# Two convolutions back to back in every second block of a fused convolution and squared-ReLU kernel

## The chip, the cores and the metric

The kernel runs on one core of a Trainium2 chip. The time is device microseconds (us) of one launch. Five engines work beside each other, each on its own in-order stream: PE (TensorE, the matmuls), ACT (ScalarE), DVE (VectorE), POOL (GpSimd) and SP (here only a queue that issues transfers). They wait for each other through semaphores. "PEld" in the profile is PE's loading of weights, which overlaps its matmuls.

## The reference, cut to what matters

Input `x` is 8 x 4096 x 192. A weight of its own for every token, head and tap (8 heads, 7 taps) goes through a softmax over the taps and then weights the token and its six predecessors (a causal dynamic convolution). The result passes through a feed-forward layer with squared ReLU.

```
w = exp(weight_gen - max);  w = w / (sum(w) + 1e-9)      # over 7 taps
out = einsum('bshk,bskhg->bshg', w, x_unf)               # x_unf: 7 shifted copies of x
h = maximum(out @ w_in, 0)                               # 192 -> 2048
y = (h * h) @ w_out                                      # 2048 -> 192
```

## The kernel before, in words

The 32768 tokens are 64 sub-blocks of 512 (`TB`). A block is two sub-blocks, apart from the first two, which are one each: 33 blocks, numbered from 0, in `BLOCKS`. A block passes through these steps.

- **Softmax pieces** (steps "E" and "S", class `Softmax`, lines 190 to 279). One batch, eight sub-blocks, is normalized at a time and in four pieces of rows, cut by `CUTS` at 0, 8, 18, 28 and 38. ACT takes the exponentials (line 238), DVE the sum, the reciprocal and the scaling (lines 245, 252, 260), and the result goes to DRAM. `TIMES` and the default in line 767 say at which unit of which block each piece is put: for a batch whose first block is `f`, at unit 9 of the blocks f-5 to f-2.
- **Rows and x** (`load_rows`, `x_load`). SP's queue loads the normalized rows (`wr`) of a block two blocks ahead; POOL's queue loads `x` (`xt`) of a block right after the conv of the block before it has been issued.
- **Bands** (step "B", `st_bands`, line 391). DVE multiplies the rows with a 0/1 mask to a banded matrix `bd`, with which the convolution becomes a matmul. A sub-block's band is one or two instructions; in block j the bands for block j+1 are made ahead of units 1 and 5.
- **Conv** (step "C", `st_conv_spread` from the ninth block on, line 464). 80 matmuls of 128 rows by 32 columns write two PSUM tiles `yp` of two banks each, 40 matmuls a tile; the first is copied to `y` by ACT, the second by DVE (line 495). Four small transfers on SP's queue then move pieces of `y` into place (line 499).
- **Units** (step "u", `st_unit`). A block has 16 units. One unit is six matmuls of 64 rows by 128 columns (line 564) into a PSUM tile `h`, a ReLU by ACT into `t1` (line 578) and a squaring by DVE into `g` (line 582). Units are squared in pairs, the last two of a block singly.
- **Second matmul** (step "M", `st_mm2`, line 613). A step is 32 matmuls: half of the 2048 inner channels for 256 tokens. Eight steps make a block. After every second step ACT copies one bank of the sum (line 627), DVE adds the other (line 629) and SP stores. The M steps of a block run while the units of the next block run: its first step needs the squares of units 0 to 7, its second those of units 8 to 15, in this order.

All tiles `yp` and `h` come from one PSUM ring of three (`ps_h`, line 89): a tile can be written when the tile three before it has been read out. The two banks of the second matmul's sum (`ps_o`) exist once: the next sum starts when DVE's addition of the last one is done.

The order is written out by hand. From the ninth block on every block follows

```
steady_spread = "MuMuuu" * 2 + "MuCMuuu" + "MuMuuu"
```

where "C" is the conv of the next block. `fill` puts the pieces E, S, B and L (load of weights) ahead of a unit. Instructions stand on each engine in the order in which these steps issue them.

Of the kernel before, what the change touches and what calls it, by code (L numbers as in the profile page):

```python
# [9 lines left out]
def kernel(  # L10
# [26 lines left out]
    nc = tc.nc  # L37
    f32 = mybir.dt.float32
    f16 = mybir.dt.float16

    B, S, D = x.shape
    H, KK = weight_gen.shape[2], weight_gen.shape[3]
# [3 lines left out]
    G = D // H  # L46
    SPREAD = H - 2
    FIRST_SPREAD = 8
    HP = H // 2

    P = 128
# [10 lines left out]
    SL = 8  # L62
# [15 lines left out]
    p_wg = ctx.enter_context(tc.tile_pool(name="p_wg", bufs=2))  # L78
    p_one = ctx.enter_context(tc.tile_pool(name="p_one", bufs=1))
    p_sm = ctx.enter_context(tc.tile_pool(name="p_sm", bufs=2))  # L80
    p_x = ctx.enter_context(tc.tile_pool(name="p_x", bufs=2))
    p_wr = ctx.enter_context(tc.tile_pool(name="p_wr", bufs=4))
    p_bd = ctx.enter_context(tc.tile_pool(name="p_bd", bufs=3))
    p_y = ctx.enter_context(tc.tile_pool(name="p_y", bufs=2))
    p_t1 = ctx.enter_context(tc.tile_pool(name="p_t1", bufs=3))
    p_g = ctx.enter_context(tc.tile_pool(name="p_g", bufs=14))
    p_os = ctx.enter_context(tc.tile_pool(name="p_os", bufs=2))
# [10 lines left out]
    mask = const.tile([P, P, 2], f16, name="mask")  # L98
    FIRST = 8
    NSEL = TB + TB - P + FIRST - 1 + P  # L100
    sel = const.tile([P, NSEL], f16, name="sel")
    PARTS = {0: (8, 8, 8, 8), 1: (8, 8, 16), 2: (16, 16)}
    v_big = const.tile([P, R + 2 * HALO, HP, SL, 2], f16, name="v_big")
    v_first = [
        const.tile([P, FIRST + 2 * HALO, HP, SL, 2], f16, name=f"v_first{i}") for i in (0, 1)
    ]

    def row_select():
# [214 lines left out]
    def x_load(j):  # L323
        x_t[j] = p_x.tile([P, NT, D], f16, name="xt")
        block_load(j, x_t[j], x[j // NBB], D, nc.gpsimd)
# [55 lines left out]
    def st_band(j, tiles):  # L381


        if j not in bd_t:
            bd_t[j] = p_bd.tile([P, H * NT * STEP], f16, name="bd")
        i = tiles[0]
        lo = STEP * i
        shift = 0 if i == 0 and j % NBB == 0 else lo - tile_start(j, i)
        n = min(STEP, P - shift)
        shape = (P, HP * len(tiles), n // SL, 2 * SL)  # L390
        nc.vector.tensor_tensor(  # L391
            out=bd_t[j][:, H * lo : H * (lo + len(tiles) * n)].rearrange(
                "p (g m c) -> p g m c", g=shape[1], c=2 * SL
            ),
            in0=wr_t[j][:, i : tiles[-1] + 1]
            .rearrange("p t g c -> p (t g) c")
            .unsqueeze(2)
            .broadcast_to(shape),
            in1=mask[:, shift : shift + n]
            .rearrange("p (m c) e -> p m (c e)", c=SL)  # L400
            .unsqueeze(1)
            .broadcast_to(shape),
            op=AluOp.mult,
        )
# [56 lines left out]
        else:  # L461
            nc.scalar.copy(out=y[:, 0:2], in_=yp)

    def st_conv_spread(j):

        s0, n = BLOCKS[j]
        y = p_y.tile([P, NK + 1, TB], f16, name="y")
        y_t[j] = y
        for ks in ((NK, NK - 1), (0, 1)):
            yp = ps_h.tile([P, 2, TB], f32, name="yp", tag="h")  # L470
            k0 = min(ks)
            for k in ks:
                for i in range(NT):
                    a, b = bounds[i], bounds[i + 1]
                    for half in (0, 1):
                        s = s0 + half
                        hi = a + (STEP if tile_start(s, i) == starts[i] else b - a)
                        bd = bd_t[s][:, H * a : H * hi].rearrange(
                            "p (g c e) -> p g e c", g=HP, e=2
                        )  # L480
                        for e in (0, 1):
                            head = 2 * k + e
                            p0 = RT * half + 32 * e
                            c0 = min(G * head, D - 32)
                            nc.tensor.matmul(  # L485
                                out=yp[p0 : p0 + 32, k - k0, a:b],
                                lhsT=x_t[s][:, i, c0 : c0 + 32],
                                rhs=bd[:, head // 2, e, 0 : b - a],
                                start=True,
                                stop=True,  # L490
                                skip_group_check=True,
                                tile_position=(0, p0),
                            )
            copy = nc.vector.tensor_copy if k0 == 0 else nc.scalar.copy
            copy(out=y[:, k0 : k0 + 2], in_=yp)  # L495
        for p0 in range(0, P, 32):
            head = SPREAD + p0 // 32 % 2
            r0 = p0 + G * head - min(G * head, D - 32)
            nc.sync.dma_start(out=y[p0 + G : p0 + 32, 0:NK], in_=y[r0 : r0 + G, NK])

    def st_conv(j):

        if j >= FIRST_SPREAD:
            return st_conv_spread(j)
        if j < NFIRST:
            return st_conv_first(j)
        y = p_y.tile([P, NK, TB], f16, name="y")
        y_t[j] = y
        yps = [ps_h.tile([P, 2 * TB], f32, name="yp", tag="h") for _ in range(2)]
        for later, s, i, q, half, a, b, base in conv_pieces(j):  # L510
            lo = bounds[i]
            hi = lo + (STEP if tile_start(s, i) == starts[i] else bounds[i + 1] - lo)
            _, ha, hb, pre = quads[q]
            m, h = (32, hb) if later else (pre, ha)
            bd = bd_t[s][:, H * lo : H * hi].rearrange("p (g c e) -> p g e c", g=HP, e=2)
            p0 = RT * half + 32 * (q % 2)
            k = q // 2
            col = TB * (k % 2) - base
            nc.tensor.matmul(  # L519
                out=yps[k // 2][p0 : p0 + m, col + a : col + b],  # L520
                lhsT=x_t[s][:, i, 32 * q : 32 * q + m],
                rhs=bd[:, h // 2, h % 2, a - lo : b - lo],
                start=True,
                stop=True,
                skip_group_check=True,
                tile_position=(0, p0),
            )
        for n, yp in enumerate(yps):
            k0, k1 = 2 * n, min(2 * n + 2, NK)
            nc.scalar.copy(  # L530
                out=y[:, k0:k1],
                in_=yp[:, 0 : (k1 - k0) * TB].rearrange("p (k c) -> p k c", c=TB),
            )
# [114 lines left out]
    with nc.allow_low_precision("fp16 matmul pipeline"), tc.manual_schedule():  # L648
# [15 lines left out]
            for j in range(first, first + P * s.r // TB):  # L664
                wr_load_sbuf(j, near, range(NT), engines)

        warm = const.tile([P, TB], f16, name="warm")
        gate = const.tile([P, 1], f32, name="gate")
        nc.vector.memset(warm, 0.0)
        nc.vector.memset(sel, 0.0)  # L670
# [43 lines left out]
        for q in range(4):  # L714
# [7 lines left out]

        steady = "MuMuuu" * 3 + "MuuuMCu"
        steady_spread = "MuMuuu" * 2 + "MuCMuuu" + "MuMuuu"
        plans = {
            0: "B1 u u u u E1 C S1 u u M u u",
            1: "L3 u u B2 M E2 B3 u M E2 u u S2 S2 u M u C u M",
# [8 lines left out]
        def at(j, u, kind, *args):  # L736
            fill.setdefault((j, u), []).append((kind, *args))
# [8 lines left out]
            (2, 0): ((6, 1), (6, 15), (7, 0)),  # L746
            (2, 1): ((7, 9), (8, 9)),
            (3, 0): ((9, 9), (10, 0), (10, 9), (11, 9)),
        }

        def exp_time(j, u):

# [10 lines left out]
        for n, s in enumerate(parts[4:], 4):  # L763
            b, f = s.b, s.fb
            k = n - min(m for m, p in enumerate(parts) if p.b == b)
            times = TIMES.get((b, k)) or (
                (f - 5, 9), (f - 4, 9), (f - 3, 9), (f - 2, 9)
            )
            assert len(times) == len(s.pieces)
            for j, u in times:  # L770
                at(*exp_time(j, u), "E", n)
                at(j, u, "S", n)
            at(times[0][0] - 1, 0, "L", n)
        for j in range(len(plans), NBLK - 1):
            a = BLOCKS[j + 1][0]
            small = [p for p in parts if p.fb <= j + 1][-1].r == FIRST
            us = {4: (7, 9), 6: (7, 9)}.get(j, (5, 9) if small else (1, 5))
            if j + 1 >= FIRST_SPREAD:
                us = (1, 5)
            for n, u in enumerate(us):  # L780
                at(j, u, "B", a + n)
        for j in range(len(plans), NBLK):
            plan, u = [], 0
            for step in steady_spread if j + 1 >= FIRST_SPREAD else steady:
                if step == "u":
                    plan += [f"{kind}{n}" for kind, n in fill.get((j, u), ())]
                    u += 1
                plan.append(step)
            plans[j] = " ".join(plan)
# [51 lines left out]

        mm2 = quarters()
        for j in range(NBLK):
            if j + 2 < NBLK:
                load_rows(j + 2)
            if j == 1:
                for q in range(WQ):
                    cross_w_in(q)
# [1 line left out]
            for step in plans[j].split():  # L850
# [4 lines left out]
                elif kind == "M":  # L855
                    next(mm2)
                elif kind == "C" and j + 1 < NBLK:
                    st_conv(j + 1)
                    if j == 0:
                        x_load(3)  # L860
                    elif j + 2 < NBLK:
                        for k in range(BLOCKS[j + 2][0], sum(BLOCKS[j + 2])):
                            x_load(k)
                    if j == 5:
                        load_w_spread()
                    elif j == 6:
# [56 lines left out]
```

The softmax here doesn't subtract the row's maximum and nothing guards it: scores larger than these inputs give would overflow.

## Time and profile before

| | us |
|---|---|
| median of three runs (732.42 to 733.91) | 733.32 |
| the profiled execution, its own time | 733.26 |
| span of the profiled execution | 731.5 |
| PE busy | 724.6 |
| DVE busy | 626.1 |
| ACT busy | 612.8 |
| POOL busy | 100.0 |

The page of the profile lists busy time by engine, the chain of work that ended last, and the costliest groups of instructions: line, engine, operation, output and input tile with their shapes, count, busy time, the mean of one, and the idle time before them with what ended it. The timeline lists merged instructions in order of time: start, duration, engine, line, tiles, count, and in brackets the idle time just before. Idle time of an engine that does not set the end costs nothing.

### The profile page before, as it was taken

What the parts mean: (1) busy time and instruction counts of PE and PEld (TensorE: products, weight loads), DVE (VectorE), ACT (ScalarE), POOL (GpSimd) and SP (SyncE); (2) the same over time, 40 slices, a digit from 0 to 9 for tenths busy, and PEclk for the clock granted to TensorE, in tenths of its full rate; (3) what the DMA queues carried; (4) which work ended last, traced back from release to release, by engine and by line L of the source; (5) the groups of instructions that cost most, each with busy time, mean ns of one, the idle gap of its engine ahead of it and who ended that gap; (6) DMA issues with size and microseconds to landing.
All of it is one profiled execution on the core that took longest, in us unless ns stands there. A gap on an engine that the chain in (4) does not pass through costs nothing.

```text
span 731.5 us, 30985 instructions
## 1 busy us (share of the span) xinstructions
PE 724.6 (99%) x14053; PEld 529.2 (72%) x14053; DVE 626.1 (86%) x834; ACT 612.8 (84%) x731; POOL 100.0 (14%) x145
## 2 busy tenths in 40 slices
PE   8999999999999999999999999999999999999998
PEld 4557788777777777777777777777777777777777
DVE  6898998998898988888988888988889988778753
ACT  5999888888888888888888888888888888888883
POOL 8232222321001100011000010010000110001000
PEclk9999999999999999999999999999999999999999
DMA  9555444784445452455433554334544315444012
GB/s 204 115 105 115 82 76 109 146 150 118 98 66 136 87 94 57 86 117 114 72 69 68 124 116 87 56 73 120 103 87 86 57 50 120 66 87 78 30 45 68
DMA packets 125984, 68.30 MB, mean 93 GB/s; under 512 B 85321, under 2 KB 122140, under 8 KB 125340
## 3 DMA queue, kind: packets, MB, share of 16 engines
q0 software_dynamic: 46192, 19.43, 22.5%
q1 hardware_dynamic: 79516, 46.79, 22.5%
q8 instruction: 110, 1.80, 1.0%
q14 instruction: 22, 0.18, 0.1%
q10 hardware_dynamic: 144, 0.10, 0.0%
HBM read 50.18 MB, written 28.70 MB: 108 GB/s over the span
## 4 chain that ended last, share of the span: by engine, by line
PE 92%; DVE 2%; issue 1%; DMA 0%; ACT 0%; DVEq 0%
PE o L613 45%; PE h L564 42%; PE yp L485 4%; PE yp L519 1%; DVE bd L391 1%; DVE g L582 1%; DMA wr<-v_first 0%; ACT t L578 0%; DVE v_first L260 0%; DVE rcp L252 0%; DVE ssum L245 0%; PE h L549 0%; DVE o_sb L629 0%; ACT o_sb L627 0%; DVEq L391 0%
## 5 line engine op out<-in xcount | busy, mean ns | idle before, releaser
L578 ACT ACTIVATE t<-h 128x1024 f16<-128x1024 f32 x512 | 496.6, 1026 | 60.3 <-PE h L564 58.9
L613 PEld LDWEIGHTS <-g 64*128 64x128 f16 (+1 forms) x8032 | 344.6, 94 | 54.9 <-issue 2.3
L613 PE MATMUL o<-w_o,g 64*128 64x192 f16 (+1 forms) x8032 | 380.4, 243 | 0.2 <-DVE o_sb L629 0.2
L582 DVE TENSOR_TENSOR g<-t 128x2048 f16<-128x2048 f16 (+1 forms) x287 | 307.4, 1105 | 28.3 <-ACT t L578 28.1
L564 PE MATMUL h<-y,w_p 64*128 64x512 f16 x2400 | 291.7, 376 | 0.0
L564 PEld LDWEIGHTS <-w_p 64*128 64x128 f16 x2400 | 113.9, 94 | 94.7
L391 DVE TENSOR_TENSOR bd<-wr,mask 128x4160 f16<-128x4160 f16 (+3 forms) x89 | 149.4, 1703 | 2.1 <-DMA wr<-v_first 1.2
L629 DVE TENSOR_TENSOR o_sb<-o,o_sb 128x384 f32<-128x384 f32 x123 | 68.4, 556 | 62.2 <-ACT o_sb L627 61.1
L321 POOL DMA_DIRECT2D xt<-in_x_dram x63 | 53.0, 844 | 415.2 <-PE yp L485 362.4
L627 ACT COPY o_sb<-o 128x384 f32<-128x384 f32 x129 | 61.7, 478 | 45.5 <-PE o L613 45.0
L564 PE MATMUL h<-y,w_i 64*128 64x512 f16 x576 | 70.8, 376 | 0.2 <-ACT y L530 0.2
L564 PEld LDWEIGHTS <-w_i 64*128 64x128 f16 x576 | 31.2, 94 | 21.4 <-issue 1.4
L485 PEld LDWEIGHTS <-xt 128*32 128x32 f16 x2000 | 24.4, 95 | 10.6 <-issue 10.6
L260 DVE TENSOR_TENSOR v_big<-ex,rcp 128x112 f16<-128x112 f32 (+5 forms) x180 | 29.9, 237 | 1.9 <-DMA vd<-v_big 0.9
L495 DVE CAST y<-yp 128x1024 f16<-128x1024 f32 x25 | 30.5, 1218 | 0.0
L485 PE MATMUL yp<-bd,xt 128*32 128x104 f16 (+1 forms) x2000 | 28.3, 210 | 0.0
L238 ACT ACTIVATE ex<-wg 128x560 f32<-128x560 f32 (+4 forms) x38 | 25.9, 683 | 2.0 <-DMA wg<-in_weight_gen_dram 2.0
L245 DVE TENSOR_REDUCE ssum<-ex 128x80 f32<-128x560 f32 (+4 forms) x38 | 25.3, 666 | 1.5 <-ACT ex L238 1.5
L495 ACT CAST y<-yp 128x1024 f16<-128x1024 f32 x25 | 25.2, 1006 | 0.0
L252 DVE RECIPROCAL rcp<-ssum 128x80 f32<-128x80 f32 (+4 forms) x38 | 22.8, 600 | 1.3
L311 POOL DMA_DIRECT2D xt<-in_x_dram x7 | 3.9, 555 | 123.8 <-PE yp L485 109.4
L351 POOL DMA_DIRECT2D wr<-v_first x24 | 12.9, 562 | 22.8 <-ACT t L578 12.2
(40 smaller groups left out, 117.2 us busy)
## 6 DMA issues: line engine op xcount, KB each, us to landing
out_dram<-o_sb SPq DMA_DIRECT2D x63, 384.0 KB
xt<-in_x_dram POOLq DMA_DIRECT2D x42, 240.0 KB, 4.8
wg<-in_weight_gen_dram SPq DMA_DIRECT2D x4, 1064.0 KB
xt<-in_x_dram POOLq DMA_DIRECT2D x21, 192.0 KB, 4.7
wr<-vd SPq DMA_DIRECT2D x38, 80.0 KB
vd<-v_big SPq DMA_DIRECT2D x5, 512.0 KB
y<-y SPq DMA_DIRECT2D x100, 24.0 KB
wg<-in_weight_gen_dram SPq DMA_DIRECT2D x3, 616.0 KB
```

The costliest lines, as they stand in the source:

```text
L238: nc.scalar.activation(out=self.ex[:, lo:hi].rearrange("p r g k e -> p (r g) k e"), in_=self.wg[:, lo:hi].rearrange("p r (g e) k -> p (r g ...
L260: eng.tensor_tensor(out=bass.AP(tensor=v.tensor, offset=v.offset + lo * H * SL + lo % SL * 2 + g * SL * 2, ap=[list(v.ap[0]), [H * SL + 2, ...
L321: eng.dma_start(out=dst[:, first:last], in_=ap)
L391: nc.vector.tensor_tensor(out=bd_t[j][:, H * lo : H * (lo + len(tiles) * n)].rearrange("p (g m c) -> p g m c", g=shape[1], c=2 * SL), in0= ...
L485: nc.tensor.matmul(out=yp[p0 : p0 + 32, k - k0, a:b], lhsT=x_t[s][:, i, c0 : c0 + 32], rhs=bd[:, head // 2, e, 0 : b - a], start=True, sto ...
L495: copy(out=y[:, k0 : k0 + 2], in_=yp)
L564: nc.tensor.matmul(out=h[:, half], lhsT=w_in_chunk(w, u, slot, half), rhs=y_t[j][r0 : r0 + RT, k], start=(slot == 0), stop=(slot == NK - 1 ...
L578: nc.scalar.activation(out=t1[:, e], in_=h, func=ActF.Relu)
L582: nc.vector.tensor_tensor(out=g[:, a : e + 1], in0=t1[:, a : e + 1], in1=t1[:, a : e + 1], op=AluOp.mult)
L613: nc.tensor.matmul(out=oo[:, cc * Dm : (cc + 1) * Dm], lhsT=g[r0 : r0 + n, cc * P : (cc + 1) * P], rhs=w_o[r0 : r0 + n, fc, :], start=(fc ...
L627: nc.scalar.copy(out=o_sb, in_=o[0][:, c])
L629: nc.vector.tensor_tensor(out=o_sb, in0=o[1][:, c], in1=o_sb, op=AluOp.add)
```

## The change

From the conv of block 15 on (`FIRST_PAIR`; the sixteenth block, counted from 0), convs come in pairs. In blocks 14, 16, ... 30 step "C" issues the convs of the next two blocks one after the other; in blocks 15, 17, ... 31 there is none. That is nine pairs. In a block with a pair the third group is "uMCMuuu" in place of "MuCMuuu". In the first conv of a pair each `yp` tile is copied to `y` in two halves, one by ACT and one by DVE; the second conv copies as before.

What the pair needs is moved ahead. The four bands of a pair (blocks c+1 and c+2, made for the pair in block c) are put ahead of units 1, 6 and 13 of block c-1 and unit 5 of block c; for the first pair, ahead of units 10 and 14 of block 13 and units 1 and 5 of block 14. The rows of the second block of a pair are loaded three blocks ahead, `x` of both blocks right after the pair before. Softmax pieces come one block earlier (f-6 to f-3), with times of their own for batch 4. Buffers grow: `xt` 2 to 4, `wr` 4 to 6, `y` 2 to 3. The bands' pool keeps its three buffers; a fourth one, `band4`, shares its memory with three tiles that are used near the start only (`sel`, `warm`, `v_first`).

```diff
+    FIRST_PAIR = 15
-    p_x = ctx.enter_context(tc.tile_pool(name="p_x", bufs=2))
-    p_wr = ctx.enter_context(tc.tile_pool(name="p_wr", bufs=4))
+    p_x = ctx.enter_context(tc.tile_pool(name="p_x", bufs=4))
+    p_wr = ctx.enter_context(tc.tile_pool(name="p_wr", bufs=6))
-    p_y = ctx.enter_context(tc.tile_pool(name="p_y", bufs=2))
+    p_y = ctx.enter_context(tc.tile_pool(name="p_y", bufs=3))
...
+    band4 = const.tile([P, H * NT * STEP], f16, name="band4")
+    VF = (FIRST + 2 * HALO) * HP * SL * 2
+    sel = band4[:, 2 * VF : 2 * VF + NSEL]
+    warm = band4[:, 2 * VF + NSEL :][:, 0:TB]
...
-            bd_t[j] = p_bd.tile([P, H * NT * STEP], f16, name="bd")
+            last = j >= BLOCKS[FIRST_PAIR][0] and (j - BLOCKS[FIRST_PAIR][0]) % 4 == 3
+            bd_t[j] = band4 if last else p_bd.tile([P, H * NT * STEP], f16, name="bd")
...
-            copy = nc.vector.tensor_copy if k0 == 0 else nc.scalar.copy
-            copy(out=y[:, k0 : k0 + 2], in_=yp)
+            if split:
+                nc.scalar.copy(out=y[:, k0 + 1], in_=yp[:, 1])
+                nc.vector.tensor_copy(out=y[:, k0], in_=yp[:, 0])
+            else:
+                copy = nc.vector.tensor_copy if k0 == 0 else nc.scalar.copy
+                copy(out=y[:, k0 : k0 + 2], in_=yp)
...
+        steady_pair = "MuMuuu" * 2 + "uMCMuuu" + "MuMuuu"
+        steady_none = "MuMuuu" * 4
...
+            (4, 0): ((12, 0), (12, 9), (13, 9), (14, 9)),
...
+        convs = {j: [j + 1] for j in range(FIRST_PAIR - 1)}
+        for j in range(FIRST_PAIR - 1, NBLK - 1):
+            convs[j] = [] if (j - FIRST_PAIR) % 2 == 0 else [j + 1, j + 2]
+        convs[NBLK - 1] = []
...
-                (f - 5, 9), (f - 4, 9), (f - 3, 9), (f - 2, 9)
+                (f - 6, 9), (f - 5, 9), (f - 4, 9), (f - 3, 9)
...
-            for n, u in enumerate(us):
-                at(j, u, "B", a + n)
+            places = [(j, u) for u in us]
+            if j + 1 >= FIRST_PAIR:
+                c = j if convs[j] else j - 1
+                if c == FIRST_PAIR - 1:
+                    places = [(c - 1, 10), (c - 1, 14), (c, 1), (c, 5)]
+                else:
+                    places = [(c - 1, 1), (c - 1, 6), (c - 1, 13), (c, 5)]
+                places = places[2 * (j - c) :][:2]
+            for n, (jb, u) in enumerate(places):
+                at(jb, u, "B", a + n)
...
-                    st_conv(j + 1)
+                    for n in convs[j]:
+                        st_conv(n, n == j + 1 and len(convs[j]) == 2)
```

## Prediction

> **What bounds the kernel now.** I read the page first (busy time, chain, groups), then the chain in order of time, then the timeline around a conv and around a block's end, then the start.
>
> ```profile
> PE 724.6 (99%) x14053; PEld 529.2 (72%) x14053; DVE 626.1 (86%) x834; ACT 612.8 (84%) x731; POOL 100.0 (14%) x145
> PE 92%; DVE 2%; issue 1%; DMA 0%; ACT 0%; DVEq 0%
> L485 PEld LDWEIGHTS <-xt 128*32 128x32 f16 x2000 | 24.4, 95 | 10.6 <-issue 10.6
> ```
>
> PE sets the end: it is busy 99% and holds 92% of the chain. DVE has 14% to spare over the whole span. The pause before a conv's first weight load is 10.6 us in all, over 25 convs.
>
> ```profile
> 400.97 1.43 PE o L613 x32
> 402.40 1.94 PE h L564 x18
> ...
> 420.03 1.32 PE o L613 x32
> 423.06 1.43 PE o L613 x32
> ```
>
> The chain gives PE's pace: three units take 1.94 us (0.65 each), an M step 1.32, the step after a conv 1.43; a block lasts 423.06 - 400.97 = 22.09. A group "MuMuuu" is 5.23. A conv so costs 22.09 - 16 x 0.65 - 8 x 1.32 = about 1.15, against 0.98 to 1.01 of weight loads for its 80 matmuls.
>
> ```profile
> 395.81 2.11 PE L564 MATMUL h<-y,w_p 64*128 64x512 f16 x18
> 396.51 0.56 DVE L629 TENSOR_TENSOR o_sb<-o,o_sb 128x384 f32<-128x384 f32 x1 [0.17 <-ACT o_sb L627]
> 396.66 2.85 ACT L578 ACTIVATE t<-h 128x1024 f16<-128x1024 f32 x3 [0.18 <-PE h L564]
> 396.99 2.31 DVE L391 TENSOR_TENSOR bd<-wr,mask 128x4160 f16<-128x4160 f16 x1
> 399.22 2.35 DVE L582 TENSOR_TENSOR g<-t 128x2048 f16<-128x2048 f16 x2
> 399.81 1.01 PEld L485 LDWEIGHTS <-xt 128*32 128x32 f16 x80 [0.42 <-issue]
> 401.49 1.22 DVE L495 CAST y<-yp 128x1024 f16<-128x1024 f32 x1
> ...
> 402.94 0.56 DVE L629 TENSOR_TENSOR o_sb<-o,o_sb 128x384 f32<-128x384 f32 x1 [0.23 <-ACT o_sb L627]
> 403.42 0.73 DVE L245 TENSOR_REDUCE ssum<-ex 128x80 f32<-128x560 f32 x1
> 404.18 0.65 DVE L252 RECIPROCAL rcp<-ssum 128x80 f32<-128x80 f32 x1
> 404.86 1.22 DVE L260 TENSOR_TENSOR v_big<-ex,rcp 128x84 f16<-128x84 f32 x8
> 406.00 2.35 DVE L582 TENSOR_TENSOR g<-t 128x2048 f16<-128x2048 f16 x2
> ...
> 408.28 0.55 DVE L629 TENSOR_TENSOR o_sb<-o,o_sb 128x384 f32<-128x384 f32 x1
> 409.37 2.52 DVE L582 TENSOR_TENSOR g<-t 128x2048 f16<-128x2048 f16 x3 [0.55 <-ACT t L578]
> 409.40 1.48 PE L613 MATMUL o<-w_o,g 64*128 64x192 f16 x32
> ...
> 411.37 1.48 PE L613 MATMUL o<-w_o,g 64*128 64x192 f16 x32
> ```
>
> This is a conv (399.81) and the end of its block (409.40). Near both, DVE works without a gap, far from its average. Two margins matter. At the conv, DVE is not free before 401.49, 1.68 after the conv's first load. At the block's end the last square is done at 409.37 + 2.52 = 411.89, and PE uses it in the last eighth of the M step at 411.37, that is at 411.37 + 7/8 x 1.32 = 412.53: 0.64 to spare. Start-to-start times on DVE, from the same lines: addition 0.48, band 2.23, pair of squares 1.13 (2.35 - 1.22), a softmax piece of ten rows 0.76 + 0.68 + 1.14 = 2.58; a single square 0.60 (0.69 long, L582 by form).
>
> **The change, part by part.**
>
> *Fewer changes between conv and unit matmuls.* Nine pairs mean nine fewer entries and exits; the 80 matmuls of each conv stay. What goes is 1.15 - 1.01 = 0.14 at least, and 0.42 (the pause) + 0.11 (1.43 - 1.32) = 0.53 at most. I take 0.25, nearer to the first, because the pause partly lies beside matmuls still running. Gain 9 x 0.25 = 2.25 us (bounds 1.3 and 4.8).
>
> *The pair and the ring of three.* Two convs write four `yp` tiles. The fourth reuses the first one's buffer, so PE stops in the middle of the second conv until ACT and DVE have both read their halves of the first. DVE's queue ahead of that half copy is today's (band ahead of unit 5, two pairs of squares), and the conv starts at the same place (unit and M step ahead of it are only exchanged), so DVE begins at +1.68 after the first load and ends 0.69 later (row of L460 below), at +2.37, plus 0.07 to hand over. PE arrives after one and a half convs, at +1.4 to +1.5. Wait 1.0 us, nine times: 9.0. Bounds: with DVE free at once, PE's half conv 0.5, 0.2 to notice, 0.59 and 0.69 for the two halves give +2.0, a wait of 0.5; a full copy's length (1.22 for 0.69) in its place gives 1.5. Behind the waiting matmul stand only PE's own next steps. The second conv's copies end some 4.3 after the first load, and the unit that needs that buffer comes after 5.6: no further stop.
>
> ```profile
> 13.08 0.59 ACT L459 CAST y<-yp 128x512 f16<-128x512 f32 x1
> ...
> 13.70 0.69 DVE L460 CAST y<-yp 128x512 f16<-128x512 f32 x1 [1.73 <-ACT y L459]
> ```
>
> This is the same kind of split copy in the first conv of the kernel: DVE idles until ACT's half ends (13.67). The built program puts the same wait on the new half copies. It costs nothing here, as ACT's half ends near +1.3, before DVE is free. [...]
>
> *The band ahead of unit 13.* In a block without conv it stands between the last addition and the last squares. Counted from the start of the last three units: addition at 0.70 (395.81 to 396.51), then 0.48 + 2.23 + 1.13 + 0.60 + 0.69, so the last square ends at 5.83. PE wants it at 1.94 + 1.32 + 0.65 + 1.16 = 5.07. PE stops 0.76 + 0.07 = 0.8 in the second M step of the next block. With a ten-row softmax piece DVE is later still: from the second group's three units, the first ReLU ends at 1.87, the squares start at 1.9, the band ahead of unit 6 at 3.03, and then all follows without a gap: 2.23 + 1.13 + 0.48 + 2.58 + 2.26 + 0.48 + 2.23 + 1.13 + 0.60 + 0.69 = 13.81, end at 16.84. PE wants it at 1.94 + 2 x 5.23 + 1.32 + 0.65 + 1.16 = 15.53: 1.4 late. Blocks 17, 21 and 25 have such a piece; an eight-row piece is about 0.6 shorter, which leaves the 0.8. So 3 x 1.4 + 5 x 0.8 = 8.2 us over blocks 15 to 29 (31 makes no bands). Bounds: 3.4 if a margin as large as today's 0.64 came on top of each, and 11.2 with 1.4 at all eight.
>
> *The transition.* Block 13 makes four bands. With the times shown: after the squares at 406.00 a band at 407.13, squares at 409.36, the addition from 410.49 to 411.05; the next block's first M step would start at 409.40: 1.7 late. Then squares 410.97, band 412.10, single squares 414.33 and 414.93 to 415.62, wanted at 412.53 + 1.7 = 414.2: 1.4 late. Together 3.1 (bounds 1 and 4).
>
> *Edits at nothing.* Pieces, rows and `x` moved ahead keep their number. `x` lands 4.8 us after its issue and is used a block or more later; POOL is 14% busy and in the waits view waits 362 us for PE before it. On SP's queue the eight `y` transfers of a pair follow each other and are wanted from the next block on, some 10 us later. If that cover were gone, the first unit of a block would wait one transfer. `warm` is cleared in 512 half-words in place of 256 words, near +0.2 at the start, under DVE's 1.5 us of idle time before the first sum (bounds 0 and 0.2).
>
> Sum: -2.25 + 9.0 + 8.2 + 3.1 = +18.05 (all low ends -4.8 + 4.5 + 3.4 + 1 = +4.1; all high ends -1.3 + 13.5 + 11.2 + 4 + 0.2 = +27.6). The profiled execution took 733.26, 0.06 below the median, so 751.3; I say 751.5.
>
> **Rivals.**
>
> 1. *DVE's spare time covers everything* (other side). For it: 14% idle, and no wait of PE for DVE above 0.2 us now. Against it: the idle time is not at these two places. It decides if the half copy is done 1.0 earlier and the last square 0.8 earlier. Then only the 2.25 is left: 731.0, 728.5 at most.
> 2. *Only the conv waits*: late squares don't reach PE, the margin at the block's end being larger than I read. 733.3 - 2.25 + 9.0 = 740, up to 743 with the transition.
> 3. *Every stop costs a restart*: PE's nearest row is the 0.42 pause. With 9 stops in convs and 2 or 3 in each of ten late M steps, some 35 x 0.42 = 14.7 more: 766. Against it: that pause is a change of matmul form, which a wait isn't.
>
> The granted clock is 9 tenths or more in all slices. [...]
>
> **How the numbers follow.** Likeliest, 745 to 759: 0.73. Smaller (rival 2 or half-size waits), 737 to 745: 0.09. Larger (rival 3), above 759: 0.13. Rival 1: 0.04 faster, 0.01 within 0.2%, which is about what a measurement of this kernel can tell from no change. The range 742 to 761 leaves out less than 0.2; its top is the sum's high end, its bottom lies between the sum's low end, 737, and the 745 of the likeliest.
>
> **What would show it.** In the second half of a pair's second conv PE waits for DVE's half copy, near 1.0 us x 9. In the blocks after 15, 17, ... the second M step waits for the line of the squares, 0.8 to 1.4, and around the end of block 13 there are two waits of 1.4 to 1.7. Two blocks last about 2 x 22.09 - 0.25 + 1.0 + 1.1 = 46.0 us in place of 44.2. The pauses before a conv's first load fall from 25 to 16. I am wrong if PE shows no wait for DVE, if it waits for a transfer, or if the clock falls.

## The result and the profile after

The changed kernel takes 755.49 us (median of four runs, 754.68 to 756.18) against 733.58 (732.42 to 733.91): a ratio of 1.030, 95% interval 1.028 to 1.032. It is 21.9 us slower; 18 were predicted, and the range of 742 to 761 holds the time. The profiled execution took 756.18 with a span of 754.5, 23.0 above the span before. All accounts below are of this span.

From the page of the changed kernel, busy times and three groups:

```profile
PE 730.2 (97%) x14053; PEld 531.6 (70%) x14053; DVE 627.9 (83%) x843; ACT 613.8 (81%) x740; POOL 99.9 (13%) x145
...
L625 PEld LDWEIGHTS <-g 64*128 64x128 f16 (+1 forms) x8032 | 344.8, 94 | 71.6 <-DVE g L594 11.1
...
L493 PE MATMUL yp<-bd,xt 128*32 128x104 f16 (+1 forms) x1640 | 28.5, 209 | 7.5 <-DVE y L504 7.5
L493 PEld LDWEIGHTS <-xt 128*32 128x32 f16 x2000 | 24.8, 95 | 14.3 <-issue 14.3
```

DVE and ACT do the same work as before, within 2 us. PE fell from 99% to 97% busy: it waits now. (The lines have new numbers: 493 and 503 to 507 are the conv and its copies, 576 the units, 594 the squares, 625 the second matmul, 641 the addition, 399 the bands.) The waits view names for whom, in total, how often, and the longest:

```profile
PEld L493 <- issue: 14.3, 27, 1.0
PEld L625 <- DVE g L594: 11.1, 25, 1.1
PEld L625 <- issue: 7.7, 10, 1.9
PE yp L493 <- DVE y L504: 7.5, 9, 0.9
...
PE o L625 <- DVE o_sb L641: 4.2, 4, 1.5
DVE bd L399 <- DMA wr<-vd: 3.7, 3, 1.8
```

PE waits for squares and for half copies, and before it waited for neither. In order of time, from the timeline of PE's weight loads, first one end of a block without conv and the conv pair after it, then the end of block 13 (its second line is a row of PE's matmuls):

```profile
443.60 0.28 PEld L625 LDWEIGHTS <-g 64*128 64x128 f16 x8 [0.18 <-DVE g L594]
444.20 0.11 PEld L625 LDWEIGHTS <-g 64*128 64x128 f16 x4 [0.32 <-DVE g L594]
444.81 0.11 PEld L625 LDWEIGHTS <-g 64*128 64x128 f16 x4 [0.49 <-DVE g L594]
454.22 1.48 PEld L493 LDWEIGHTS <-xt 128*32 128x32 f16 x121 [0.16 <-issue]
456.64 0.45 PEld L493 LDWEIGHTS <-xt 128*32 128x32 f16 x35 [0.94 <-issue]
457.74 0.10 PEld L493 LDWEIGHTS <-xt 128*32 128x32 f16 x4 [0.65 <-issue]
```

```profile
302.20 1.25 PEld L625 LDWEIGHTS <-g 64*128 64x128 f16 x30 [1.83 <-issue]
302.20 1.48 PE L625 MATMUL o<-w_o,g 64*128 64x192 f16 x31 [1.47 <-DVE o_sb L641]
306.17 0.12 PEld L625 LDWEIGHTS <-g 64*128 64x128 f16 x4 [1.08 <-DVE g L594]
306.77 0.11 PEld L625 LDWEIGHTS <-g 64*128 64x128 f16 x4 [0.49 <-DVE g L594]
```

In the first group, the first three lines are one second M step that gets its last squares one by one, 0.99 us late in all. The pair then runs without a pause through 121 of its 160 loads and waits 0.94 for the half copy. The last pause, 0.65 before the last four loads of the pair, has no releaser: "issue". It was not expected. What DVE did in the meantime:

```profile
439.62 0.56 DVE L641 TENSOR_TENSOR o_sb<-o,o_sb 128x384 f32<-128x384 f32 x1
440.10 2.32 DVE L399 TENSOR_TENSOR bd<-wr,mask 128x4160 f16<-128x4160 f16 x1
442.33 2.42 DVE L594 TENSOR_TENSOR g<-t 128x2048 f16<-128x2048 f16 x3
...
453.63 2.35 DVE L594 TENSOR_TENSOR g<-t 128x2048 f16<-128x2048 f16 x2
455.90 1.28 DVE L504 CAST y<-yp 128x512 f16<-128x512 f32 x2
```

Addition, band, three squares without a gap; and the half copy at 455.90, 1.68 after the conv's first load at 454.22, as the queue ahead of it allows. At the end of block 13 the first wait is "issue" in the row of the weight loads; the row of the matmuls names its cause, DVE's addition, which frees the bank of the sum.

Adding up the idle times of PE's weight loads from the end of block 13 on, with the pauses before the first load of a conv left out:

| wait | us |
|---|---|
| second half of the second conv, nine pairs (0.92 to 0.99 each) | 8.6 |
| late squares after blocks 15 to 29 (three times 1.6, five times 0.8 to 1.0) | 9.5 |
| end of block 13 | 3.4 |
| one M step whose bank came free late, at 616.8 | 1.4 |
| two "issue" pauses of 0.65 in the fourth and eighth pair | 1.3 |
| sum | 24.2 |

One wait lies ahead of all these, where convs are not yet paired. DVE waits for the rows of a band, its addition comes late, and the M step behind it waits for the bank:

```profile
134.99 2.33 DVE L399 TENSOR_TENSOR bd<-wr,mask 128x4160 f16<-128x4160 f16 x1 [1.80 <-DMA wr<-vd]
138.97 1.48 PE L625 MATMUL o<-w_o,g 64*128 64x192 f16 x31 [1.50 <-DVE o_sb L641]
```

The kernel before has no such wait there; the conv of block 14 starts at 289.36 in it and at 290.93 here, so 1.6 of the 23.0 us are lost before block 13 ends. All kernels with pairs but the one with moved seams (below) show this wait of DVE, 1.0 to 2.2 us. The edits that reach this stretch are the larger buffers and the shared `band4`; POOL issues a group of its loads of `x` and of weights at 105.59 there, and at 121.45 before. Which of this makes the rows late was not tried.

### The profile page after: what moved, and what is told of

Its sections match the earlier page's. It is cut to its first block, busy times and chain, and to the rows that moved or that the text cites. A ratio compares the mean times of both kernels' runs of the same rounds, so it can differ in the third digit from the quotient of the medians.

```text
span 754.5 us, 30959 instructions
## 1 busy us (share of the span) xinstructions
PE 730.2 (97%) x14053; PEld 531.6 (70%) x14053; DVE 627.9 (83%) x843; ACT 613.8 (81%) x740; POOL 99.9 (13%) x145
## 5 line engine op out<-in xcount | busy, mean ns | idle before, releaser
L625 PE MATMUL o<-w_o,g 64*128 64x192 f16 (+1 forms) x8032 | 385.7, 243 | 10.0 <-DVE g L594 4.8
L576 PE MATMUL h<-y,w_p 64*128 64x512 f16 x2400 | 290.6, 376 | 0.0
L576 PEld LDWEIGHTS <-w_p 64*128 64x128 f16 x2400 | 115.4, 94 | 95.8
L399 DVE TENSOR_TENSOR bd<-wr,mask 128x4160 f16<-128x4160 f16 (+3 forms) x75 | 128.5, 1736 | 6.0 <-DMA wr<-vd 3.7
L576 PE MATMUL h<-y,w_i 64*128 64x512 f16 x576 | 70.8, 376 | 0.2 <-ACT y L542 0.2
L576 PEld LDWEIGHTS <-w_i 64*128 64x128 f16 x576 | 31.7, 94 | 21.0 <-issue 1.4
L507 DVE CAST y<-yp 128x1024 f16<-128x1024 f32 x16 | 19.5, 1222 | 3.0 <-PE yp L493 3.0
L358 POOL DMA_DIRECT2D wr<-band x24 | 13.0, 560 | 64.8 <-DVE band L267 50.4
L399 DVE TENSOR_TENSOR band<-wr,mask 128x3328 f16<-128x3328 f16 (+2 forms) x14 | 21.0, 1531 | 0.0
```

The costliest lines, as they stand in the source:

```text
L399: nc.vector.tensor_tensor(out=bd_t[j][:, H * lo : H * (lo + len(tiles) * n)].rearrange("p (g m c) -> p g m c", g=shape[1], c=2 * SL), in0= ...
L576: nc.tensor.matmul(out=h[:, half], lhsT=w_in_chunk(w, u, slot, half), rhs=y_t[j][r0 : r0 + RT, k], start=(slot == 0), stop=(slot == NK - 1 ...
L625: nc.tensor.matmul(out=oo[:, cc * Dm : (cc + 1) * Dm], lhsT=g[r0 : r0 + n, cc * P : (cc + 1) * P], rhs=w_o[r0 : r0 + n, fc, :], start=(fc ...
```

## The experiments

Each runs beside the kernel before on the same chip, which took 732.99 to 733.45 there.

**The band ahead of unit 13**

```diff
-                    places = [(c - 1, 1), (c - 1, 6), (c - 1, 13), (c, 5)]
+                    places = [(c - 1, 1), (c - 1, 6), (c, 1), (c, 5)]
```

> One edit against the changed kernel: the band ahead of unit 13 of a block without conv goes ahead of unit 1 of the block after it; the conv pairs, the split copies and the first pair's bands stay. Theory (the band between the last addition and the last squares makes PE wait at the block's end): the waits of the second M step for the squares in the eight blocks after blocks 15 to 29, 9.5 us together in the trace of the changed kernel, go; the two at the end of block 13 (3.4 us) and the waits in the convs (8.6 us) stay: 755.5 - 9.5 = 746.0. Rival (DVE simply has too much to do over a pair of blocks, and the place does not matter): the band now delays DVE in the block of the pair, the conv's wait grows by about as much, and the time stays within 2 us of 755.5.

Measured: 748.02 (746.71 to 749.99), a ratio of 1.020 (1.018 to 1.022); the span is 746.3, 8.2 below that of the changed kernel. In the waits view one line is left of the squares, the two waits at the end of block 13:

```profile
PEld L625 <- DVE g L594: 1.6, 2, 1.1
```

The waits at the eight block ends are gone, and the waits in the convs stay at 0.93 to 1.00. So the place of the band, not DVE's load, made PE wait. The time fell by 7.5 and not 9.5, though the wait of 1.4 at 616.8 is gone as well. The "issue" pauses, 1.3 before, are 1.9 here, and 1.0 us more is lost ahead of the pairs, where nothing was edited: the conv of block 14 starts at 291.90 here and at 290.93 in the changed kernel.

**The split copies**

```diff
-                        st_conv(n, n == j + 1 and len(convs[j]) == 2)
+                        st_conv(n)
```

> One edit against the changed kernel: the first conv of a pair copies its two tiles as the second does, the first tile whole by ACT, the second whole by DVE. Theory (the fourth tile of a pair waits for DVE's half copy, which stands behind two pairs of squares): ACT's whole copy of 1.0 us starts 0.7 after the conv's first load and ends at 1.7, PE arrives at 1.4, so the wait falls from 0.95 to 0.35: 755.5 - 9 x 0.6 = 750.1, and PE's wait names ACT in place of DVE. Rival (the ring of three is what costs, and any copy is late by as much): no change beyond 1 us.

Measured: 754.39 (753.25 to 756.16), a ratio of 1.029 (1.027 to 1.031), 1.1 less than the changed kernel where 5.4 were expected. The wait for the copy did fall as expected, from 0.94 to between 0.28 and 0.36 in all nine pairs. But other pauses stand in or just behind six of them; four lines of PE's weight loads, the first a wait for the copy:

```profile
454.90 0.46 PEld L493 LDWEIGHTS <-xt 128*32 128x32 f16 x35 [0.29 <-issue]
456.91 0.10 PEld L493 LDWEIGHTS <-xt 128*32 128x32 f16 x4 [1.55 <-issue]
...
504.95 0.19 PEld L625 LDWEIGHTS <-g 64*128 64x128 f16 x5 [1.06 <-issue]
...
642.26 0.14 PEld L493 LDWEIGHTS <-xt 128*32 128x32 f16 x8 [1.61 <-issue]
```

The second line is the 0.65 of the changed kernel, four loads before the end of the same pair, now 1.55. Such pauses add up to 5.6 us here, against 1.3. Neither of the two theories had them.

**The rows of a pair's first block**

```diff
-                ahead = 3 if n > FIRST_PAIR and not convs[n - 1] else 2
+                ahead = 3 if n > FIRST_PAIR else 2
```

> One edit against the changed kernel: the rows of the first block of a pair are loaded three blocks ahead as those of the second are, not two. Theory (where a batch starts, those rows are loaded at the start of the block in which their band stands ahead of unit 1, and the band came 1.5 to 1.9 us late, which cost PE one wait of 1.4 us): DVE no longer waits for the rows and that one wait goes: 755.5 - 1.4 = 754.1. Rival (the lateness is absorbed, the wait of PE there has another cause): 755.5.

Measured: 756.34 (755.87 to 756.94), no less than the changed kernel. DVE still waits 2.7 us for rows in two places. One of them is the wait ahead of the pairs (1.8), which this edit doesn't touch; at the batch's start 0.9 is left of 1.9. PE's wait behind it is 0.3 in place of 1.4, and the time doesn't show it; the "issue" pauses grew from 1.3 to 2.2. A miss: DVE's wait did not go, since at a batch's start the load waits for the store of the last softmax piece, wherever it stands (the store is issued at 602.87, the load at 607.97).

**All three edits**

> The three edits together: band ahead of unit 1 of the pair's block, whole copies in both convs, rows three blocks ahead; the convs stay back to back. Theory: what is left against the kernel before is the saving of nine changes of matmul form (the changed kernel's span less its waits gives 754.5 - 24.3 = 730.2, which is 1.3 under the span before), 9 x 0.35 of waits in the convs, and 3.4 at the end of block 13: 733.6 - 1.3 + 3.2 + 3.4 = 738.9. Rival (the pairing costs something beyond these waits): 742 or more. Other rival (the waits hide each other, so that removing all three frees more than the sum): 735 or less.

Measured: 745.86 (744.01 to 746.3), a ratio of 1.016 (1.015 to 1.018); 738.9 was expected. The first rival is right: the pairing costs something beyond the three waits. Where it lies can be counted out. A pair takes 1730 instructions of PE to the next pair (each matmul has its weight load as an instruction of its own), 62 short of seven times 256, and the first pair starts at PE's instruction 11845 in the built program. Counting loads from there, the pauses of the second and of this experiment lie at the instructions 12227, 15555, 17347, 19139, 24259 and 26051. All leave the same remainder on division by 256: 195 (why it is 195 and not 0 is not shown). The pairs two and six, where such a point falls near the middle of the pair, have none. In pair seven it falls on the wait for the copy, which is 0.90 there and 0.28 to 0.31 in the others.

The page of this and of every kernel here has a line for the queue that brings instructions:

```profile
q8 instruction: 110, 1.80, 1.0%
```

110 packets of 1.80 MB are 16.4 KB each, and PE's 28144 instructions in the built program fill 110 pieces of 256. So PE's instructions come in pieces of 256, and the pauses stand at the seams. The times of these packets in the traces agree. In the kernel with all three edits one packet runs from 452.06 to 452.98, and the pause of 1.81 ends at 454.38, 1.40 later. All six pauses there end 1.37 to 1.48 us after the end of such a packet, and those of the other kernels with pairs 1.2 to 1.6. All six stand where more than three quarters of a piece of 256 belong to two convs back to back: 320 instructions pass there in about 2 us, while an M step has 64 in 1.32.

**Moving the seams**

If this is right, 64 more instructions at the start must move the pauses by one pair.

```diff
         spin(21)
+        for i in range(32):
+            nc.tensor.matmul(out=wp[:, 0:64], lhsT=warm[:, 0:P], rhs=warm[:, 0:64], start=True, stop=True)
```

> e4_three with 32 small matmuls (64 PE instructions) more behind the warming matmuls at the start, otherwise the same. A pair takes 1730 PE instructions, 62 short of a multiple of 256, so the ends of 256 move by one pair. Theory (instructions): the unexplained pauses move with them. e4_three has them in the pairs 1 (0.2), 3 (0.6), 4 (1.8), 5 (0.3), 7 (0.6), 8 (1.3) and 9 (1.0) and hardly any in 2 and 6; here they are expected in 1 (about 1.2), 2 (0.2), 4 (0.5), 5 (1.6), 6 (0.7), 8 (0.6), 9 (1.4), with 3 and 7 nearly free. Rival (the pauses belong to what happens at those times, transfers or stores): they stay in the pairs 3, 4, 5, 7, 8 and 9. The time is that of e4_three plus up to 3 us at the start.

Measured: 745.22, one run. The pauses at the seams, first in the kernel with all three edits (pairs 1, 4, 5, 8, 9), then here (pairs 1, 2, 5, 6, 9), from the timelines of PE's weight loads:

```profile
320.41 0.09 PEld L625 LDWEIGHTS <-g 64*128 64x128 f16 x1 [0.23 <-issue]
...
454.38 0.10 PEld L493 LDWEIGHTS <-xt 128*32 128x32 f16 x4 [1.81 <-issue]
...
500.30 0.19 PEld L625 LDWEIGHTS <-g 64*128 64x128 f16 x5 [0.32 <-issue]
...
634.64 0.14 PEld L493 LDWEIGHTS <-xt 128*32 128x32 f16 x8 [1.26 <-issue]
...
681.11 0.36 PEld L625 LDWEIGHTS <-g 64*128 64x128 f16 x9 [1.00 <-issue]
```

```profile
319.97 0.09 PEld L493 LDWEIGHTS <-xt 128*32 128x32 f16 x1 [1.46 <-issue]
...
365.92 0.10 PEld L625 LDWEIGHTS <-g 64*128 64x128 f16 x2 [0.29 <-issue]
...
499.21 0.11 PEld L493 LDWEIGHTS <-xt 128*32 128x32 f16 x5 [1.53 <-issue]
...
545.25 0.26 PEld L625 LDWEIGHTS <-g 64*128 64x128 f16 x6 [0.52 <-issue]
...
678.80 0.16 PEld L493 LDWEIGHTS <-xt 128*32 128x32 f16 x9 [1.32 <-issue]
```

The small pause behind the first pair is now behind the second (0.23 and 0.29, one or two loads before an M step's end), the long one of the fourth pair is in the fifth, that of the eighth in the ninth, and the third and seventh are free. Not all sizes came as expected: the fourth pair, put at 0.5, has hardly any pause. Apart from the start nothing else was changed, and transfers and stores are issued in the same order. The pauses belong to places in PE's stream of instructions, not to moments.

**Back to back or apart, with no wait for copies**

Both of the next two copy only a part of the first conv's result, so that the copies cost next to nothing:

```diff
             if split:
-                nc.scalar.copy(out=y[:, k0 + 1], in_=yp[:, 1])
-                nc.vector.tensor_copy(out=y[:, k0], in_=yp[:, 0])
+                nc.scalar.copy(out=y[:, k0 : k0 + 2, 0:64], in_=yp[:, :, 0:64])
+                nc.gpsimd.memset(y[:, k0 : k0 + 2, 64:], 0.0)
```

and one of them takes the convs apart:

```diff
-        steady_pair = "MuMuuu" * 2 + "uMCMuuu" + "MuMuuu"
+        steady_pair = "MuMuuu" * 2 + "uMCMCuuu" + "MuMuuu"
...
-                    for n in convs[j]:
-                        st_conv(n, n == j + 1 and len(convs[j]) == 2)
+                    todo = [n for n in convs[j] if n not in y_t]
+                    st_conv(todo[0], len(todo) == 2)
+                    if len(todo) == 2:
+                        continue
```

> As e5_apart with the same short copies and zeros in the first conv's y, but with the two convs back to back. No wait for copies is left in the convs. Theory (instructions): the pauses at the 256 instruction ends grow to 6 or 7 us, since the 0.3 us waits that covered a part of them are gone: 733.5 - 1.3 to 2.2 for the saved form changes + 3.4 + 6.5 = 741 to 742, slower than e5_apart by 3 to 4. Rival (no such supply limit): 735, faster than e5_apart by the nine form changes and its 0.9 of small waits.

> Against e4_three: an M step stands between the two convs of a pair (uMCMCuuu in place of uMCMuuu), and the first conv's tiles are copied only in their first 64 columns of 512, by ACT; POOL clears the rest of y, so that half of the blocks from 15 on work on mostly zeros. PE's instructions keep their number. Theory (beyond the waits for copies, PE waits for its own instructions: in the trace of e4_three the pauses that no engine explains, 5 us, all stand where 256 instructions end, and only where nearly all of those 256 belonged to two convs back to back): with an M step between, such pauses are gone. 733.5 with the old number of form changes, plus 3.4 at the end of block 13 and about 0.9 of small waits: 737.8, faster than e6_short. Rival (the pauses come with the copies or the rows, not with the density of instructions): they stay here, 742.

Measured: back to back 745.98 (743.30 to 749.35, a wide spread), apart 742.73 (742.21 to 743.35), where 741 to 742 and 737.8 were expected. The order of the medians is the one expected, but the two profiled spans are equal, 741.6, so that the difference is not sure. Back to back, the pauses at the seams are 7.3 us, near the 6 or 7 expected (up to 1.62, below), though no copy is waited for. Apart, they are not gone but 2.9 (up to 0.78, below): 256 instructions can still hold 192 of the two convs' 320 when an M step of 64 stands between. Taken apart, the units behind the second conv wait 0.2 for the ring again and again (5.0 us before L576 in all, against 1.6), which was put at 0.9.

From the kernel back to back, two lines from the third and fourth pair, then from the one apart:

```profile
403.89 1.55 PEld L493 LDWEIGHTS <-xt 128*32 128x32 f16 x125 [0.16 <-issue]
...
452.19 0.10 PEld L493 LDWEIGHTS <-xt 128*32 128x32 f16 x4 [1.62 <-issue]
```

```profile
453.76 0.47 PEld L493 LDWEIGHTS <-xt 128*32 128x32 f16 x36 [0.78 <-issue]
```

The kernel back to back also prices the saved change of form by itself. Its second pair has no pause of any kind, and from there to the start of the third 403.89 - 359.94 = 43.95 us pass; the kernel before needs 2 x 22.09 = 44.18. That is 0.23 a pair, 2.1 for nine; the sixth pair, without a pause too, gives the same 43.95. The first line of the stretch:

```profile
359.94 1.92 PEld L493 LDWEIGHTS <-xt 128*32 128x32 f16 x160 [0.16 <-issue]
```

**Apart, with whole results**

The convs apart as above but with whole copies, the band and the rows as in the kernel with all three edits, and the first pair's bands moved:

```diff
-                    places = [(c - 1, 10), (c - 1, 14), (c, 1), (c, 5)]
+                    places = [(c - 1, 13), (c, 0), (c, 1), (c, 5)]
```

> The result is whole again: the pair with an M step between its convs, whole copies in both, band ahead of unit 1 of the pair's block, rows three blocks ahead, and the first pair's bands ahead of unit 13 of block 13 and units 0, 1 and 5 of block 14 in place of 10, 14, 1 and 5. Theory: no instruction pauses, no conv waits, and of the 3.4 at the end of block 13 about half stays (0.8 late squares once, and small ones): 733.5 + 1.7 + 0.7 = 736. Rival (the end of block 13 is not due to the four bands there): 737.8. If the time falls to 733 or below, moving work ahead is worth something by itself, which neither theory says.

Measured: 741.57 (740.47 to 742.65), a ratio of 1.011 (1.010 to 1.013), against 736. The part on block 13 holds: the waits of 3.4 there are 1.8 here (0.28, 0.33, 0.49 and 0.70). The rest is what the kernel apart showed: 3.7 at the seams, 1.1 behind late rows, and the units that wait 0.2 for the ring. Moving the work ahead bought nothing.

**A conv behind an M step, without pairs**

```diff
-        steady_spread = "MuMuuu" * 2 + "MuCMuuu" + "MuMuuu"
+        steady_spread = "MuMuuu" * 2 + "uMCMuuu" + "MuMuuu"
```

> One edit against the kernel before, not the changed one: the third group of every block from the ninth on is uMCMuuu in place of MuCMuuu, so each single conv follows an M step as the pairs do, and not a unit; nothing is paired. In the trace of the kernel before, each of 25 convs starts after a pause of 0.42 us in PE's weight loads; in every kernel with pairs the conv that follows an M step starts after 0.16. Theory (part of what the pairs save is the place after an M step, not the saved form change): 0.1 to 0.26 less for each of 25 convs, 733.3 - 2.5 to 6.5 = 727 to 731. Rival (the pause is only displaced, as the M step's own last matmuls run 0.2 longer, and what the pairs save is the one form change less): 733.3, no change.

Measured: 733.12 against 733.02, a ratio of 1.0001 (0.9992 to 1.0010). The pause before a conv is 0.16 in place of 0.42, as in the pairs, the M step ahead of it lasts 0.18 longer, and the time is the same: the rival is right.

```profile
400.00 0.98 PEld L485 LDWEIGHTS <-xt 128*32 128x32 f16 x80 [0.16 <-issue]
```

The length of that pause is therefore not the price of a change of form: it shrank by 0.26 with as many changes as before, and the time stayed.

**x behind the rows**

```diff
-                        for n in next((convs[c] for c in range(j + 1, NBLK) if convs[c]), ()):
+                        for n in next((convs[c] for c in range(j + 1, NBLK) if convs[c]), ())[:1]:
...
+            if j >= FIRST_PAIR - 1:
+                for n in next((convs[c] for c in range(j, NBLK) if convs[c]), ()):
+                    for k in range(BLOCKS[n][0], sum(BLOCKS[n])):
+                        if k not in x_t:
+                            x_load(k)
```

> Against e3_rows_ahead: x of the second block of a pair is loaded at the start of the next block, not right behind x of the first. Theory (where a batch starts, its rows come late because their store lands late: four x transfers in a row were issued just ahead of it): DVE's waits for rows (2.7 us in two places in e3_rows_ahead) fall under 0.5. The time is about that of e3_rows_ahead, 756.3, less 0 to 1. Rival (the store and the load are slow by themselves): the waits stay between 2 and 3.5 us.

Measured: 756.21 (755.30 to 756.65); DVE's waits for rows stay at 2.4 us. Of these, 1.6 is the wait ahead of the pairs, which this edit doesn't reach; at the batch's start 0.8 is left, against 0.9 with the rows ahead. So the `x` transfers are hardly what makes those rows late. In the traces of this experiment and of the one with the rows ahead the store is issued about 0.6 after its softmax piece is done, since SP is still issuing the eight `y` transfers of the pair (597.0 to 602.7, where the kernel before has four in 2.8 us), and the load follows 4.6 to 5.1 us later. Whether those eight are the cause was not tried.

## Why the prediction was right

The prediction's terms, against the idle times of the changed kernel and the experiments. Idle time before a weight load is not quite what PE loses, so a second column has the delay, read from when the next step starts. An M step that waits for nothing takes 1.45 us from its first load to the next step's; the one at 489.10 takes 2.87. A pair that waits for nothing takes 2.0 (in the kernel back to back); here a pair takes 3.0, and two of the nine, with a seam, 3.7.

| term | predicted | idle | delay | shown by |
|---|---|---|---|---|
| saved changes of form | -2.25 | -2.1 | -2.1 | 43.95 against 44.18 for two blocks |
| wait for the first conv's half copies | 9.0 | 8.6 | 9.3 | the copy whole: 0.94 falls to 0.3 |
| band ahead of unit 13 | 8.2 | 9.5 | 8.5 | the band moved: gone, time -7.5 |
| bands at the end of block 13 | 3.1 | 3.4 | 3.2 | the bands moved: 1.8 left |
| rows late at a batch's start | 0 | 1.4 | 1.2 | wait at 616.8; not confirmed in the time |
| instructions late at seams | not named | 1.3 | 1.3 | seams moved: the pauses move |
| rows late ahead of the pairs | 0 | 1.9 | 1.6 | conv of block 14 at 290.93, not 289.36 |
| sum | 18.05 | 24.0 | 23.0 | span +23.0 |

By delay the terms make up the whole difference of the spans. The four terms that were named come to 18.9, so the sum was not right by errors that cancel; the other 4.1 had been put at nothing or not named.

*The two waits.* Both chains of durations, taken row by row from the kernel before, gave the waits to a tenth: a half copy at +1.68, a wait of 1.0 (0.92 to 0.99 measured as idle time), block ends late by 0.8 and 1.4 (0.84 and 1.42 by delay). As idle time the block ends show up to 0.2 more, 0.8 to 1.0 and 1.6: PE gets the squares in three pieces and stops three times. Two blocks were put at 46.0 us and took 45.8 to 47.1. That the copies run one after the other was of no matter, as written: DVE was late by itself.

*The gain.* 0.25 a pair was a choice between 0.14 and 0.53, and 0.23 is what came; that it came so near is partly luck. My reason for it, that the pause of 0.42 partly lies beside running matmuls, fits the single convs behind an M step: there the pause shrinks by 0.26, and the time doesn't move.

*What failed.* Two things, and one bound. "Edits at nothing" held for the rows' number, not for their time: at one batch's start their band waited 1.9 us for them, and PE 1.4 behind it, and ahead of the pairs the same cost 1.6. And the part on the pair named one thing that a second conv right behind the first runs into, the ring of three, and not the supply of instructions. In the changed kernel, where a pair also waits 0.92 to 0.99 for the copy, this is a small term, 1.3 us. With that wait at 0.3 it is 5.6 us and without it 7.3, more than twice what the pairing can gain. Rival 3, a restart cost at every stop, did not come: the delays make up the span. The granted clock stayed at 0.999 to 1.0 in all profiled runs: it did not fall. The bound is the low end of the band's term: 8.2 less eight margins of 0.64 is 3.1, not 3.4, and the low end of the sum +3.8, not +4.1.

*No better version.* None of the variants with pairs is below the kernel before. The two convs back to back can save 2.1 us, and even without any wait for copies the seams cost 7.3.

## What to carry to other kernels

Where one engine is busy all the time, the spare time of another is of use only where it lies: ask of a moved instruction what stands behind it in its own queue and when the bound engine wants that, and add up the rows between, rather than compare busy shares. When a wait is removed and the time does not follow, look for pauses without a releaser and count instructions between them: a common remainder shows a limit that no engine's row names. And dense runs of tiny matmuls can outrun the supply of instructions: 320 PE instructions in 2 us did so here, while the 160 of a single conv, in 1.1, did not.

## What the runs showed of the hardware beyond what was expected

- PE's instructions arrive in pieces of 256 (110 packets of 16.4 KB for 28144), and a piece that is used up fast is waited for: back to back with no wait for copies, PE paused behind pieces that were used up in 1.5 to 2.6 us and not behind those that took 2.9 or more. Over all kernels that show such pauses, a piece and the pause behind it took 2.5 to 3.9 us together. In the kernel with a single conv behind an M step, 256 instructions took no less than 3.1, and no pause is seen.
- Back to back with no wait for copies, a pause differs with the place of the seam: 1.5 to 1.6 where the seam lies four to eight loads before the end of the pair, 0.9 to 1.2 where it lies 23 to 27 loads behind the pair and 0.6 at 31, 0.6 to 0.8 where it lies near the middle of the second conv, and none near the start of the second conv.
- The pause before a conv's first weight load is 0.42 us behind a unit and 0.16 behind an M step, which then lasts 0.18 longer, at the same total time (733.12 against 733.02).
